# A build-time list scheduler for a fused chunk-attention and swish-MLP kernel, with other staging, transposes and rings for parts of its input

## The chip, the cores and the metric

The kernel runs on one core of one Trainium2 chip. The metric is device time in microseconds (us), median of several executions. The profile adds one execution that the hardware profiler recorded. An execution that is over 1.5% slower than the fastest of the same kernel is called slow here. Engines: PE is TensorE (matmul), PEld its weight load, DVE is VectorE, ACT is ScalarE, POOL is GpSimd, SP is SyncE. SP and ACT start DMA transfers; "SPq" is SP's instruction queue.

## The reference, cut to what matters

```
q, k, v: (8, 8, 576, 64) float32;  w_in: (512, 2048);  w_out: (2048, 512);  beta: (2048,)
# attention inside chunks of 64 positions
scores = 1/sqrt(64) * q_c @ k_c^T ;  attn = softmax(scores) ;  out = attn @ v_c
x = out.transpose(0, 2, 1, 3).reshape(4608, 512)
# MLP
h = x @ w_in
g = h * (1 / (1 + exp(-beta * h)))
y = g @ w_out                      # (4608, 512) float32
```

## The kernel before

The 4,608 tokens are nine blocks of 512. Block b is half-blocks 2b and 2b+1, so there are 18 half-blocks, 0 to 17. For each half-block: load q, k and v, cast them to bf16, transpose q and k, `scores`, `exp`, `attend`, normalize, transpose x. For each block: `mm1` (x times w_in, 16 tiles), `gate` (ACT and DVE), `mm2` (g times w_out, 16 tiles for each of four groups of 128 tokens), `keep_y` and the store. The attention of a later block and `mm2` of the block before are woven into `mm1` of a block.

Every engine has one queue that is fixed when the kernel is built and runs in order. An operation waits on semaphores for what it reads and for buffers that it overwrites, and everything behind it in that queue waits too. The order comes from a table of times written by hand:

```python
        events = []
        def at(time, fn, *args, **kw):
            events.append((time, len(events), fn, args, kw))
        def rest(h, tc, tt_, to, tv, ts, tx):          # attention with DMA transposes
            for w in range(2):
                at(tc + 1.0 * w, cast_qk, h, w, "pool")
                at(to + 2.0 * w, order, h, w, "pool")  # qkT -> qkO
            at(tt_, turn_dma, h)                       # on SP: qkb -> qkT
            ...
            at(ts, scores, h)
            ...
            at(tx, turn_x_dma, h)                      # on SP: xn -> xT
        for j in range(3):
            at((17, 20, 23)[j], load_w_out, j)         # into wstage, after w_in's casts
        ...
        events.sort(key=lambda e: (e[0], e[1]))
```

q and k of half-blocks 0 to 3 are transposed on PE, of all later ones by a DMA that SP starts (`turn_dma`); POOL then copies `qkT` to `qkO` in another order, and PE's `scores` reads `qkO`. The last block gathers the tails of eight sequences, so each of its two half-blocks needs 20 small loads instead of 6. And the output's DMAs are started by ACT.

The softmax here doesn't subtract the row's maximum and nothing guards it: scores larger than these inputs give would overflow.

## Time and profile before

The time was 360.49 us (median of 3, 357.36 to 363.85).

| from the profile before | |
|---|---|
| profiled span | 360.0 us |
| PE busy | 291.3 us (81%) |
| longest PE gap | 17.88 us, waiting for `qkO` |

The first lines of the page: busy time with share of the span, then PE, the granted clock and DMA in 40 equal slices, as tenths.

```profile
PE 291.3 (81%) x2466; PEld 142.1 (39%) x2498; DVE 141.2 (39%) x255; ACT 148.5 (41%) x230; POOL 122.6 (34%) x126
...
PE   1688977698696799999699969996999009899996
...
PEclk9999999899989999999789989998999757999999
DMA  8996999990962299269626962695244491312123
```

PE is the busiest engine, but it dips once in each block, and in slices 32 and 33 it does nothing. DMA, nearly full for the first 81 us, has a share of only about a half after that. So bandwidth is not, on the whole, what holds PE back after the start; waits are.

Waits of SP's queue and of PE: engine, line, what it waited for, total us, times, longest.

```profile
SPq L426 <- DVE g L464: 94.4, 11, 13.4
...
SPq L426 <- DVE xn L409: 23.8, 3, 13.3
```

```profile
PE A L370 <- POOL qkO L213: 26.3, 5, 17.9
```

SP stands for 94 us and 24 us before transposes of x (L426), and all loads behind them stand with it. PE loses 26 us to `qkO`, most of it once. The timelines of PE and SP show that once (start, duration, engine, line, operation; in brackets the idle time before it and what ended it):

```profile
278.04 1.03 PE L444 MATMUL F<-xT,w_in_bf 128*128 128x512 bf16 x4
296.95 0.64 PE L370 MATMUL A<-qkO 64*64 64x64 bf16 x32 [17.88 <-POOL qkO L213]
```

```profile
253.78 8.46 SPq L426 DMA_TRANSPOSE xT<-xn  x2
262.28 5.90 SPq L265 DMA_DIRECT2D qkstage<-in_q_dram  x8
268.22 5.72 SPq L265 DMA_DIRECT2D qkstage<-in_k_dram  x8
273.98 5.68 SPq L265 DMA_DIRECT2D qkstage<-in_q_dram  x8
279.71 5.69 SPq L265 DMA_DIRECT2D qkstage<-in_k_dram  x8
285.43 2.71 SPq L281 DMA_DIRECT2D vstage<-in_v_dram  x4
288.19 4.98 SPq L341 DMA_TRANSPOSE qkT<-qkb  x2
```

The last block's loads start only after the transposes of x, and SP needs 0.72 us for each. The transpose of q and k comes behind 36 of them at 288.2, POOL's copies come after it, and PE stands still until 297.

### The profile page before, as it was taken

The numbers are of one execution on the slowest core, as the hardware profiler recorded it, in microseconds if no ns is written. First come the engines' busy times: TensorE is split into PE (matmuls) and PEld (weight loads), VectorE is DVE, ScalarE is ACT, GpSimd is POOL, SyncE is SP. The second block draws the span as 40 slices with busy tenths as digits, with TensorE's granted clock in tenths as the row PEclk, the third lists the DMA queues.
The fourth block names the chain that finished last, engine by engine and source line by source line (L and its number), as shares of the span: only waits on it lengthen the run. The fifth ranks groups of instructions, "written<-read, shape, count | busy, mean of one in ns | idle before, by whom it ended". The sixth has DMA issues, their size and how long they took to land.

```text
span 360.0 us, 6004 instructions
## 1 busy us (share of the span) xinstructions
PE 291.3 (81%) x2466; PEld 142.1 (39%) x2498; DVE 141.2 (39%) x255; ACT 148.5 (41%) x230; POOL 122.6 (34%) x126
## 2 busy tenths in 40 slices
PE   1688977698696799999699969996999009899996
PEld 0563434475242344434243424343434004344444
DVE  1438631585125633453145415432543003534300
ACT  2437323684225635544344434343445003535421
POOL 1735362492180057314901480149002165000000
PEclk9999999899989999999789989998999757999999
DMA  8996999990962299269626962695244491312123
GB/s 228 352 353 198 348 304 251 216 267 8 184 132 58 69 268 219 59 175 270 142 53 159 275 158 59 196 271 119 60 121 120 128 196 33 78 32 56 31 58 87
DMA packets 101594, 57.54 MB, mean 160 GB/s; under 512 B 84024, under 2 KB 85312, under 8 KB 101568
## 3 DMA queue, kind: packets, MB, share of 16 engines
q1 hardware_dynamic: 93712, 47.33, 53.3%
q10 hardware_dynamic: 7856, 9.84, 10.3%
q8 instruction: 19, 0.31, 0.4%
q14 instruction: 7, 0.06, 0.1%
HBM read 36.71 MB, written 9.44 MB: 128 GB/s over the span
## 4 chain that ended last, share of the span: by engine, by line
PE 40%; DMA 16%; SPq 12%; DVE 12%; ACT 7%; POOL 5%; issue 3%; ACTq 3%; DVEq 0%
PE F L477 19%; PE F L444 11%; DMA qkT<-qkb 10%; DVE g L464 6%; SPq L265 6%; SPq L257 6%; POOL qkO L213 5%; DVE xn L409 3%; DMA qkstage<-in_k_dram 3%; ACT tt L461 3%; PE F L448 3%; ACTq L496 3%; PE A L444 3%; ACT E L379 3%; PE A L370 2%
## 5 line engine op out<-in xcount | busy, mean ns | idle before, releaser
L464 DVE SCALAR_TENSOR_TENSOR g<-tt,F 128x512 bf16<-128x512 bf16 (+1 forms) x148 | 91.8, 628 | 166.7 <-ACT tt L461 165.6
L477 PE MATMUL F<-w_out_bf,g 128*128 128x512 bf16 (+1 forms) x560 | 142.0, 381 | 5.8 <-issue 2.2
L461 ACT ACTIVATE tt<-F,beta_half 128x512 bf16<-128x512 f32 (+1 forms) x148 | 93.5, 641 | 127.0 <-PE F L444 104.4
L444 PE MATMUL F<-xT,w_in_bf 128*128 128x512 bf16 x448 | 117.9, 390 | 9.8 <-DVE g L464 6.4
L477 PEld LDWEIGHTS F<-w_out_bf,g 128*128 128x128 bf16 x592 | 56.3, 99 | 65.3 <-issue 3.5
L213 POOL CAST qkb<-qkstage 128x1024 bf16<-128x1024 f32 x33 | 34.2, 1040 | 117.0 <-DMA qkstage<-in_q_dram 90.6
L444 PEld LDWEIGHTS F<-xT,w_in_bf 128*128 128x128 bf16 x448 | 42.9, 100 | 69.5 <-DVE g L464 15.8
L213 POOL COPY qkO<-qkT 128x1024 bf16<-128x1024 bf16 x28 | 53.6, 1952 | 32.2 <-DMA qkT<-qkb 32.2
L370 PE MATMUL A<-qkO 64*64 64x64 bf16 x576 | 9.8, 208 | 34.2 <-POOL qkO L213 26.3
L379 ACT ACTIVATE E<-A 128x1024 bf16<-128x1024 f32 (+1 forms) x22 | 19.0, 865 | 34.0 <-PE A L370 34.0
L207 ACT ACTIVATE ostage<-F 128x512 f32<-128x512 f32 (+1 forms) x36 | 21.3, 591 | 23.0 <-PE F L477 20.4
L213 POOL CAST v_bf<-vstage 128x512 bf16<-128x512 f32 x36 | 21.6, 619 | 14.4 <-DMA vstage<-in_v_dram 14.1
L448 PE MATMUL F<-xT,w_in_bf 128*128 128x256 bf16 x160 | 23.2, 301 | 3.1 <-DVE g L464 1.7
L409 DVE TENSOR_TENSOR xn<-A,R 128x512 bf16<-128x512 f32 x36 | 24.9, 692 | 1.2
L370 PEld LDWEIGHTS A<-qkO 64*64 64x64 bf16 x576 | 7.2, 119 | 42.3 <-POOL qkO L213 28.8
L448 PEld LDWEIGHTS F<-xT,w_in_bf 128*128 128x128 bf16 x160 | 15.9, 106 | 7.5 <-DVE g L464 2.1
L407 DVE RECIPROCAL R<-A 128x8 f32<-128x8 f32 x36 | 7.2, 201 | 17.3 <-PE A L395 17.3
L444 PE MATMUL A<-xT,w_in_bf 128*128 128x512 bf16 x48 | 11.0, 380 | 1.7 <-DVE w_in_bf L213 1.7
L395 PEld LDWEIGHTS A<-v_bf,E 64*64 64x64 bf16 x576 | 7.3, 119 | 11.6 <-ACT E L379 4.1
L395 PE MATMUL A<-v_bf,E 64*64 64x65 bf16 x576 | 9.8, 208 | 2.2 <-ACT E L379 2.2
L323 PE MATMUL F<-ident,qkb 128*128 128x128 bf16 x32 | 4.2, 312 | 8.0 <-DVE qkb L213 8.0
L461 ACT ACTIVATE tt<-A,beta_half 128x512 bf16<-128x512 f32 x12 | 8.2, 687 | 3.3 <-PE A L444 3.3
(34 smaller groups left out, 64.0 us busy)
## 6 DMA issues: line engine op xcount, KB each, us to landing
out_dram<-ostage ACTq DMA_DIRECT2D x70, 128.0 KB, 3.4
qkstage<-in_q_dram SPq DMA_DIRECT2D x32, 256.0 KB, 5.2
qkstage<-in_k_dram SPq DMA_DIRECT2D x32, 256.0 KB, 5.2
vstage<-in_v_dram SPq DMA_DIRECT2D x30, 256.0 KB, 6.0
wstage<-in_moe_w_out_dram SPq DMA_DIRECT2D x4, 1024.0 KB, 7.5
wstage<-in_moe_w_in_dram SPq DMA_DIRECT2D x3, 1024.0 KB, 12.2
wstage<-in_moe_w_in_dram SPq DMA_DIRECT2D x2, 512.0 KB
qkstage<-in_q_dram SPq DMA_DIRECT2D x16, 64.0 KB
```

The costliest lines, as they stand in the source:

```text
L207: P.op("act", lambda e: e.activation(dst, src, AF.Copy, **kw), reads, writes)
L213: P.op(eng, lambda e: e.tensor_copy(dst, src), reads, writes, rows)
L257: return e.dma_start(qkstage[:, s, which, hb, :], src[blk][heads, 256 * hv:256 * hv + 256, :].rearrange("h (t i) d -> t h (i d)", i=8))
L265: return e.dma_start(qkstage[32 * c:32 * c + 32, s, which, hb, :], src[4 * hv + c][heads, S - 64:S, :].rearrange("h (t i) d -> t h (i d)", ...
L370: return e.matmul(bank(hb)[64 * c2:64 * c2 + 64, 64 * i:64 * i + 64], qkO[r, s, 1, hp, 64 * c:64 * c + 64], qkO[r, s, 0, hp, 64 * c:64 * c ...
L379: P.op("act", lambda e: e.activation(E[:, s, :, a:b, :].rearrange("p g i q -> p g (i q)"), A[:, 0:2, 64 * a:64 * b], AF.Exp, scale=0.125), ...
L409: P.op("dve", lambda e: e.tensor_tensor(xn[:, s, u, :, :, :].rearrange("p c k (h d) -> p c (k h) d", h=2), o[:, :, :, 0:64], R[:, 2 * u:2 ...
L444: return e.matmul(bank(n).rearrange("p (v c t) -> p v c t", v=2, c=4), w, xT[:, sx, :, u, :, 64 * hb:64 * hb + 64], start=(kt == 0), stop= ...
L448: return e.matmul(bank(n)[:, 256 * hv:256 * hv + 256].rearrange("p (c t) -> p c t", c=4), w, xT[:, sx, hv, u, :, 64 * hb:64 * hb + 64], st ...
L461: P.op("act", lambda e: e.activation(tt[:, T % 3, c], bank(n)[:, c], AF.Tanh, scale=beta_half[:, t:t + 1]), reads=[K("ps", n, v=("h", blk, ...
L464: P.op("dve", lambda e: e.scalar_tensor_tensor(g2[:, sg, t, c], tt[:, T % 3, c], 1.0, bank(n)[:, c], ALU.add, ALU.mult), reads=[K("ps", n, ...
L477: P.op("pe", lambda e, t=t: e.matmul(bank(n)[:, 0:b - a], g2[:, sg, t, 128 * s:128 * s + 128], w_out_bf[:, t, a:b], start=(t == 0), stop=( ...
```

## The change: its intent and the diff

The intent is to replace the times written by hand by a list scheduler that runs when the kernel is built. Each call gets a rank; loads and DMA transposes of q and k also form a "line" whose order is kept. The scheduler models every engine, the two DMA rings and the 16 DMA engines with fixed durations, lets each engine take the ready operation of lowest rank, and the order that results is the order of the queues. The chip still runs fixed queues; the model decides nothing at run time.

The diff, cut to its core (the long rest turns `at(...)` into `go(...)` and adds a duration to every operation; the `#` comments and the `...` at the ends of lines are put in here):

```diff
-        events.sort(key=lambda e: (e[0], e[1]))
-        for _, _, fn, args, kw in events:
-            fn(*args, **kw)
-        P.finish("sp")
+        P.schedule()        # list scheduling: "us" below are its modelled durations
         P.build()
 ...
+            P.dma("sp", (2.5, 128, 27), lambda e: e.dma_start_transpose(      # turn_dma
+                P.dma(queue, (0.62, 2, 92), lambda e, c=c: e.dma_start(       # last block's q, k
+            P.dma(queue, (0.6, 4, 92), lambda e: e.dma_start(                 # put
 ...
+        def stage_w_out(j):                                  # (a) was wstage[:, j]
+            if j == 0:
+                return vstage[:, 1, :, :, :].rearrange("p n h d -> p (n h d)"), ...
+            if j == 1:
+                return qkstage[:, 2, :, :, :].rearrange("p w b x -> p (w b x)"), ...
+            t0 = 8 * (j - 2)
+            return g2[:, 1, t0:t0 + 8, :].rearrange("p t d -> p (t d)").bitcast(F32), ...
 ...
+        load_half(0, "sp", "act")                            # (b) two rings
+        load_half(1, "sp", "act")
 ...
-        rest(4, 51, 53.2, 57.7, 57.5, 62, 65.5)
-        rest(5, 53, 57, 62, 61.8, 66.2, 69.5)
+        for h in (4, 5):                                     # (c) block 2 turned on PE
+            attention(h, "pe", (A0, A1), None, ("act", "dve"))
 ...
+        def stage_qk(h):                                     # (d) last block into wstage
+            if h < 2 * LAST:
+                return qkstage[:, h % NQ, :, :, :], ...
+            s = h % 2
+            return wstage[:, s, :].rearrange("p (w b x) -> p w b x", w=2, b=2), ...
 ...
+            at = None if h < 6 else 1000 + 10 * (h - 2)      # (e) load_half: place in SP's line
 ...
+                load(turn_dma, h, at=995 + 10 * h)           # its transposes, in the same line
 ...
+                go(r, scores, h, (0, 1), slack=0.5)
 ...
-        NOS = 3
+        NOS = 5                                              # output tiles in flight
 ...
+                go(0.5, put, blk, s, j, "sp")                # (f) stores from SP, were on ACT
```

A `slack` makes the model treat an operation's input as that much later than it is, so the operation gets a later place in its queue. It adds no wait.

## The prediction

> **What bounds the kernel now.** TensorE (PE) and the waits that starve it. In the table of busy time by stretch and PE's timeline, four 512-column matmuls start every 0.865 us in dense stretches, so 1,152 equivalents need about 249 us. Attention and PE transposes add about 18 us (estimate). The span is 360 us. The loss by stage:
>
> - blocks 0 and 1, 19.7 to 99.4 us: 80 us for about 58 us of PE work. DMA share 0.93, then 0.83. The w_out loads wait for the w_in staging buffers (issued 17.5 to 33 us, the fourth at 37); the data rate falls from about 350 to 198 GB/s. PE waits 3.2 us for transposed x at 99.4;
> - block 2, 99.4 to 126.8 us: 27 us for about 18.5;
> - blocks 3 to 6: 31, 36, 35 and 36 us; block 7: 48; block 8: 30; each has 27.7 us of matmuls plus about 1 us of attention. The DMA queue's waits show why: SP is in order, and the transposes of x wait 94 us in total behind gates of an earlier block, holding back the next loads. The largest PE gap is 17.9 us (279 to 297), waiting for qkO; in the chain, SP issues the last block's small loads one after another at 0.72 us. The clock there falls to 0.82; dense stretches run at 1.00. The Trainium skill, "TensorE: Matmul & The Clock Gate" (Part 1), says that idling halves the clock and activity restores it; the trace agrees (0.50 after that gap, 1.00 later), so filling gaps also removes slow matmuls.
>
> **What the change does.** It removes no matmul. (a) w_out gets its own staging, so loads stream without that gap. (b) The first two half-blocks load on two rings. The skill, "DMA: Bandwidth & Descriptors", says both share the same 16 engines, so I expect 1 to 2 us. (c) Block 2 is turned on PE: +1.6 us of PE, against DMA transposes of 4.5 to 7.3 us and POOL copies of 1.95 us. (d) The last block's 40 loads go into free staging well ahead: removes nearly all of the 17.9 us. (e) Loads no longer sit behind blocked transposes: removes 2.5 to 8 us in each of blocks 3 to 7. (f) Output issues leave ACT (0.6 us each) and go to SP.
>
> **Sum (estimates from the durations above).** Loads through half-block 5 plus both weights are about 17 MB; DMA takes until about 57 us. Block 2 starts near 80 (was 99.4), block 3 near 100 (was 126.8). Six blocks at 29.2 us end at 275. Final matmuls 14, last store 4: 293. I add 9 us of stalls, because a static order made from modelled durations drifts from real ones, and DMA would be busy about 25 us of each 29: **302 us, range 290 to 318**. Faster by over 2%: 0.96; within 2%: 0.03; slower: 0.01.
>
> **What would show it.** Block 2's first mm1 near 80 us; blocks 3 to 8 at 28.5 to 30.5 us each; no PE gap over 3 us after 100 us; PE waits on qkO falling from 26 us to under 4; PE busy over 90% of the span; mean clock 0.97 or more; no 94 us of x-transpose waits; w_out issued without the gap.
>
> **What would make it wrong.** DMA near saturation stretching transposes so that PE waits for x every block (then 320 to 335); an SP order that differs from real readiness; early loading slower than estimated; or better, if stalls are near zero (about 290).

## The result, and the profile after

The kernel with the change took **321.98 us** (median of 4, 320.96 to 323.29), against 359.83 (4 runs, 357.36 to 363.85) for the kernel before in the same rounds. The ratio is 0.897, 95% interval 0.891 to 0.903. A ratio is the mean time of one kernel's fast runs over that of the other's fast runs of the same rounds, so it is not quite the ratio of the medians quoted. The change is 38 us faster, and 20 us slower than predicted, outside the range.

```profile
PE 289.6 (90%) x2546; PEld 144.0 (45%) x2546; DVE 143.4 (45%) x263; ACT 152.5 (47%) x241; POOL 114.4 (36%) x119
...
PE   0679998998999999899999999599399999999994
...
PEclk9999999999999999999999999879779999999999
DMA  6999199989999999999999559539901521111133
```

PE's busy time is the same as before, its idle time fell from 68.7 to 31.9 us. The dips of each block are gone, but slices 26 and 29 (5 and 3 tenths) are new holes, with a lower clock around them, and DMA has a hole in slice 5 (1 tenth).

The same stretch table for the kernel after; columns are the stretch, its length, busy us (and instructions) of PE, PEld, DVE, ACT, POOL, then the granted clock, DMA share and GB/s:

```profile
core 0: us, PE busy (x) PEld busy (x) DVE busy (x) ACT busy (x) POOL busy (x), PEclk, DMA share, GB/s
32.00:40.00 8.00, 8.00 (x39) 3.63 (x37) 7.08 (x15) 5.05 (x8) 2.35 (x4) 1.00 0.09 33
...
199.00:235.00 36.00, 26.65 (x193) 11.34 (x192) 10.17 (x17) 12.01 (x18) 15.94 (x12) 0.83 0.71 144
235.00:322.00 87.00, 82.45 (x484) 38.45 (x482) 30.55 (x48) 35.55 (x54) 0.00 (x0) 0.99 0.22 49
```

From 199 to 235 us PE idles 9.4 us and is granted 0.83 of its clock, with DMA far from full. After that PE is nearly always busy. The waits of SP and of PE:

```profile
SPq L641 <- ACT ostage L319: 64.2, 16, 9.7
SPq L482 <- POOL v_bf L321: 32.7, 11, 5.5
SPq L253 <- POOL w_out_bf L321: 13.8, 1, 13.8
...
SPq L385 <- DVE w_out_bf L321: 4.4, 1, 4.4
```

```profile
PE A L513 <- POOL qkO L321: 9.3, 2, 5.7
PE F L468 <- DVE qkb L321: 8.3, 1, 8.3
```

SP's 94 us before transposes of x are gone; it now waits to start stores (L641), most of it late in the kernel, when little else is left to issue (62 of the 64 us come after 222 us), and for w_out's casts early on. The 32.7 us at L482, the transposes of q and k, were there before as well (32.1 us). The list puts them down to POOL's cast of v, on which the kernel does not make a transpose depend; such releasers are inferred, and what holds these issues stays open. PE's waits for `qkO` fell from 26.3 to 9.3 us, in two gaps; the other line, 8.3 us, is the very start of the kernel. PE's timeline at the two gaps:

```profile
202.79 1.03 PE L591 MATMUL F<-xT,w_in_bf 128*128 128x512 bf16 x4
207.43 0.64 PE L513 MATMUL A<-qkO 64*64 64x64 bf16 x32 [3.61 <-POOL qkO L321]
208.00 1.89 PE L620 MATMUL F<-w_out_bf,g 128*128 128x512 bf16 x4
...
223.78 1.03 PE L591 MATMUL F<-xT,w_in_bf 128*128 128x512 bf16 x4
230.54 0.64 PE L513 MATMUL A<-qkO 64*64 64x64 bf16 x32 [5.73 <-POOL qkO L321]
```

The two operations that wait are `scores` of half-blocks 15 and 16. After each gap four matmuls take 1.89 us instead of 1.03: PE runs at half clock until 212.8 and 236.7. And this is what SP did while PE came to the first gap:

```profile
171.00 5.95 SPq L482 DMA_TRANSPOSE qkT<-qkb  x1
176.99 1.24 SPq L641 DMA_DIRECT2D out_dram<-ostage  x2
178.27 3.06 SPq L391 DMA_DIRECT2D wstage<-in_q_dram  x4
181.37 2.82 SPq L391 DMA_DIRECT2D wstage<-in_k_dram  x4
184.23 1.27 SPq L573 DMA_TRANSPOSE xT<-xn  x1
185.55 0.68 SPq L391 DMA_DIRECT2D wstage<-in_q_dram  x1
186.27 1.16 SPq L641 DMA_DIRECT2D out_dram<-ostage  x2
187.48 2.23 SPq L391 DMA_DIRECT2D wstage<-in_q_dram  x3
189.75 2.82 SPq L391 DMA_DIRECT2D wstage<-in_k_dram  x4
192.61 0.68 SPq L405 DMA_DIRECT2D wstage<-in_v_dram  x1
193.34 1.34 SPq L573 DMA_TRANSPOSE xT<-xn  x1
194.73 1.32 SPq L641 DMA_DIRECT2D out_dram<-ostage  x2
196.09 2.05 SPq L405 DMA_DIRECT2D wstage<-in_v_dram  x3
198.18 3.38 SPq L482 DMA_TRANSPOSE qkT<-qkb  x1
```

SP hardly waits for data here. The last cast that transpose 14 reads ended at 161.2 us, and that of transpose 15 at 175.8, 22 us before its issue (the casts in the order of POOL's queue). Between the transposes of half-blocks 14 (171.0) and 15 (198.2) it starts 20 loads of the last block (14.3 us), six stores (3.7 us) and two transposes of x (2.6 us). The next 20 loads stand in the same way before transpose 16 at 221.8. From its issue to `scores` transpose 15 needs 9.2 us (5.3 for the DMA, 3.8 for POOL's two copies), so `scores` of 15 starts at 207.4. PE had reached it at 203.8.

To see where time is lost, I took the start times of all matmuls and subtracted from each step the time that this kind takes in dense stretches (0.216 us for 512 columns, 0.108 for 256, 0.056 for 128, 0.0084 for the small ones of attention). This "loss" holds waits and half-clock time alike:

| stage, after | work, us | loss, us |
|---|---|---|
| before the first matmul | | 8.3 |
| 8.3 to 80.7 us | 52.8 | 19.8 |
| 80.7 to 199 us | 111.8 | 6.4 |
| 199 to 235 us | 21.3 | **14.9** |
| 235 us to the last matmul | 80.6 | 1.2 |
| all | 266.5 | 50.6, and 4.2 after the last matmul |

Of the 14.9 us, 9.7 come before `scores`; nearly all of the rest is half clock. The Trainium skill, "TensorE: Matmul & The Clock Gate" (section "Why this matters for your kernels"), says to leave no PE idle gap above about 3 us between bursts, or the clock falls. The traces agree in kind: the 3.61 us gap was followed by 5.3 us of slow matmuls, and the one 2.0 us gap of run e1 below by none. But in the kernel before, gaps of 2.76, 2.69 and 2.57 us (ending at 175.7, 211.9 and 246.8 us) were each followed by half clock too, so 3 us is not a safe limit.

### The profile page after: what moved, and what is told of

Read it like the earlier page. It is cut to its first block, busy times and chain, and to the rows that moved or that the text cites. A ratio compares the mean times of both kernels' runs of the same rounds, so it can differ in the third digit from the quotient of the medians.

```text
span 321.5 us, 6150 instructions
## 1 busy us (share of the span) xinstructions
PE 289.6 (90%) x2546; PEld 144.0 (45%) x2546; DVE 143.4 (45%) x263; ACT 152.5 (47%) x241; POOL 114.4 (36%) x119
## 4 chain that ended last, share of the span: by engine, by line
PE 80%; DVE 6%; DMA 6%; POOL 2%; ACT 2%; SPq 2%; issue 1%; DVEq 0%
PE F L620 37%; PE F L591 27%; PE F L595 4%; DVE xn L552 3%; PE A L591 3%; DMA qkT<-qkb 3%; PE A L513 3%; POOL qkO L321 2%; PE A L538 2%; DMA qkstage<-in_q_dram 2%; PE A L560 1%; PE A L468 1%; PE F L468 1%; DVE g L611 1%; DVE R L550 1%; ACT E L522 1%
## 5 line engine op out<-in xcount | busy, mean ns | idle before, releaser
L591 PE MATMUL F<-xT,w_in_bf 128*128 128x512 bf16 x448 | 113.4, 384 | 2.0 <-DVE g L611 1.9
L620 PEld LDWEIGHTS F<-w_out_bf,g 128*128 128x128 bf16 x592 | 57.0, 99 | 65.3 <-issue 3.3
L591 PEld LDWEIGHTS F<-xT,w_in_bf 128*128 128x128 bf16 x448 | 42.4, 99 | 55.6 <-DVE g L611 9.5
L321 POOL COPY qkO<-qkT 128x1024 bf16<-128x1024 bf16 x24 | 46.4, 1964 | 22.4 <-DMA qkT<-qkb 18.4
L321 POOL CAST qkb<-qkstage 128x1024 bf16<-128x1024 f32 x30 | 30.8, 1044 | 28.8 <-DMA qkstage<-in_q_dram 22.6
L319 ACT ACTIVATE ostage<-F 128x512 f32<-128x512 f32 (+1 forms) x36 | 21.3, 592 | 33.1 <-PE F L620 33.1
L321 POOL CAST v_bf<-vstage 128x512 bf16<-128x512 f32 x32 | 19.7, 617 | 25.7 <-DMA vstage<-in_v_dram 25.3
L522 ACT ACTIVATE E<-A 128x512 bf16<-128x512 f32 (+1 forms) x24 | 19.4, 810 | 17.5 <-PE A L513 17.5
L595 PE MATMUL F<-xT,w_in_bf 128*128 128x256 bf16 x160 | 22.0, 289 | 0.0
L595 PEld LDWEIGHTS F<-xT,w_in_bf 128*128 128x128 bf16 x160 | 15.6, 104 | 2.7
L321 POOL CAST qkb<-wstage 128x1024 bf16<-128x1024 f32 x4 | 4.2, 1042 | 20.7 <-DMA wstage<-in_q_dram 15.5
```

The lines of the kernel that those rows point to most:

```text
L319: P.op("act", us, lambda e: e.activation(dst, src, AF.Copy, **kw), reads, writes)
L321: P.op(eng, us, lambda e: e.tensor_copy(dst, src), reads, writes)
L522: P.op("act", act_us(128 * (b - a)), lambda e: e.activation(E[:, s, :, a:b, :].rearrange("p g i q -> p g (i q)"), A[:, 0:2, 64 * a:64 * b] ...
L591: return e.matmul(bank(n).rearrange("p (v c t) -> p v c t", v=2, c=4), w, xT[:, sx, :, u, :, 64 * hb:64 * hb + 64], start=(kt == 0), stop= ...
L595: return e.matmul(bank(n)[:, 256 * hv:256 * hv + 256].rearrange("p (c t) -> p c t", c=4), w, xT[:, sx, hv, u, :, 64 * hb:64 * hb + 64], st ...
L620: P.op("pe", 0.2158 * (b - a) / 512, lambda e, t=t: e.matmul(bank(n)[:, 0:b - a], g2[:, sg, t, 128 * s:128 * s + 128], w_out_bf[:, t, a:b] ...
```

## The experiments

Theory A: PE's queue holds `scores` of half-blocks 15 and 16 earlier than their `qkO` can exist, because SP's in-order queue issues their transposes late, behind the last block's loads and the stores; the static order, made with shorter modelled times, turns SP's lateness into PE waits. Rivals: the data are late because DMA is short of bandwidth; the hole at 32 to 40 us starves the rest; PE's own order does not matter because what follows needs the same data anyway.

Running only the kernel's own scheduler shows its belief: it places `scores` of 15 at 198.8 and of 16 at 213.1 us, and a span of 300.4 us. That is a plan and no measurement; the chip ran them at 207.4 and 230.5. Where a run below is said to change the order of a queue, the queues that the two kernels' schedulers build were compared in this way too.

### e5_late_scores: PE's order, for three operations

```diff
-                go(r, scores, h, (0, 1), slack=0.5)
+                go(r, scores, h, (0, 1), slack={15: 6, 16: 13, 17: 6}.get(h, 0.5))
```

> Only the place of three groups of score matmuls (half-blocks 15, 16, 17) in PE's fixed order changes; no load, transpose or output is touched. Theory A (PE's order, made from a model that has the transposes of q and k some 9 and 17 us too early, waits although other matmuls are ready): the gaps of 3.6 and 5.7 us before the scores and the two half-clock stretches of 6.8 us go, and the time falls by 13 to 17 us, to about 305 to 309 us. Theory B (DMA is saturated there, so that data are truly late for the block that needs them): the wait only moves to a later matmul and the time stays within 3 us of 322.

Measured: **309.84 us** (309.25 to 310.21), ratio 0.862 [0.856, 0.868]. The fall of 12.1 us is a little less than the 13 to 17 expected. In the queues, what moved is these scores with what hangs on them (`exp`, `attend`, normalize and the transposes of x) and one group of `mm2`; loads, stores and transposes of q and k keep their order among themselves. The transposes were issued nearly as late (195.9 and 219.1 us). PE now does other matmuls first. The first line is PE's `scores` of 15, without a wait; the second is the stretch table:

```profile
210.79 0.45 PE L513 MATMUL A<-qkO 64*64 64x64 bf16 x32
```

```profile
199.00:235.00 36.00, 36.00 (x257) 16.33 (x256) 15.64 (x25) 18.90 (x29) 15.04 (x11) 1.00 0.63 137
```

The loss from 199 to 235 us fell from 14.9 to 0.6 us, and 12 us of time went with it. So the data were in time for what needs them; only the order made PE wait. The bandwidth rival falls, and so does the one that says that PE's order doesn't matter.

### e1_turn_first: SP's order

```diff
             at = None if h < 6 else 1000 + 10 * (h - 2)
+            if h >= 2 * LAST:
+                at = 996 + 10 * (h - 1)
```

This puts transposes 15 and 16 ahead of the last block's loads.

> The transposes of half-blocks 15 and 16 are issued ahead of the last block's 20 loads each, instead of behind them. Theory A (loads of the last block, about 0.72 us each on the in-order SP queue, hold the transposes back): transpose 15 is issued near 178 us instead of 198, the first gap (3.6 us) and its half-clock stretch go; transpose 16 is issued near 203 instead of 222, so the second gap shrinks to 0 to 4 us; time 307 to 315 us. Theory B (saturated DMA): the transposes land no earlier, both gaps stay, 319 to 324 us.

Measured: **314.89 us** (311.57 to 316.5; the run of 316.5 is slow, and the median of the other three is 314.07), ratio 0.877 [0.870, 0.885]. SP's timeline, transposes 15 to 17:

```profile
180.31 2.21 SPq L482 DMA_TRANSPOSE qkT<-qkb  x1
202.37 2.66 SPq L482 DMA_TRANSPOSE qkT<-qkb  x1
226.50 3.01 SPq L482 DMA_TRANSPOSE qkT<-qkb  x1
```

Transpose 15 comes 18 us earlier than in the change, 16 comes 19 us earlier. What is left is one wait of 2.0 us, before `scores` of 17. PE's queue changed here too: the scheduler, which now expects the data sooner, puts `scores` of 15 and 16 earlier (behind 748 and 820 matmuls of the MLP, 788 and 852 in the change), and still PE does not wait for them. The lateness can be cured from either end, on SP or on PE.

### e6_old_stage: undo the staging of step (d)

```diff
-            if h < 2 * LAST:
+            if True:
```

in `stage_qk` and `stage_v`, so the last block uses the old buffers.

> The last block is staged in the buffers of the other blocks again, as before the change; the order of all queues stays. If the free staging is what moved its loads up, they start later than 178 us and the largest gap grows again by 5 us or more (327 us and up). If the order of the SP queue sets their time (they start at 178 us though the staging is free from about 36 us), nothing changes: 320 to 324 us, the same gaps of about 3.6 and 5.7 us.

Measured: 323.48 us (321.08 to 324.35), ratio 0.899, waits for `qkO` 9.7 us, no difference that the runs resolve. The scheduler builds the same five queues, operation for operation. The free staging alone did nothing: the loads' place in SP's line, and not a free buffer, set their time. In the change the last cast out of `wstage` ends at 32.4 us, yet the loads start at 178.3.

### e8_recal: measured costs in the scheduler's model

```diff
-            P.dma("sp", (2.5, 128, 27), lambda e: e.dma_start_transpose(
+            P.dma("sp", (3.8, 128, 27), lambda e: e.dma_start_transpose(
-                P.dma(queue, (0.62, 2, 92), lambda e, c=c: e.dma_start(
+                P.dma(queue, (0.72, 2, 92), lambda e, c=c: e.dma_start(
```

and alike for the other loads (from 0.62 to between 0.65 and 0.72) and the stores (0.60 to 0.64).

> Only numbers of the build-time model change: what one issue on SP costs, set to what the trace after the change shows (transposes of q and k 3.8 us instead of 2.5, loads of the last block 0.72 instead of 0.62, other loads 0.65 to 0.70, outputs 0.64 instead of 0.60). The list scheduler then orders the same work by itself. Theory A (the order is bad because these costs were too low): the model's own times of the last three score groups move 7 to 11 us later, PE no longer waits over 2 us for qkO after 190 us, 307 to 312 us. If the issue costs are not what misled it, the gaps of 3.6 and 5.7 us stay: 318 to 323 us.

Measured: 315.9 us (314.81 to 316.33), ratio 0.880 [0.874, 0.886]. One wait of 4.3 us for `qkO` stays, that of half-block 15. This misses the expectation: right mean costs give half of the gain. The new plan has `scores` of 16 and 17 11 us later, but those of 15 only 1.0 us later (199.8 instead of 198.8), which fits the wait that stays. The model still knows nothing of SP's issues that are held up: single loads that mostly take 0.60 us took up to 3.43 us while DMA was full, and the transposes ranged from 2.0 to 5.95 us.

### e4_wout_own: the early hole in DMA

The hole at 32 to 40 us: w_out's pieces 0 and 1 borrow buffers of half-block 2, so its loads wait for w_out's casts (the lines of 13.8 and 4.4 us above; SP idles from 20.2 to 38.5 us).

```diff
             if j == 0:
-                return vstage[:, 1, :, :, :]...
+                return qkT[:, :, :, :, :].rearrange("p s w i t -> p (s w i t)").bitcast(F32), ...
             if j == 1:
-                return qkstage[:, 2, :, :, :]...
+                return ostage[:, 0:4, :].rearrange("p n d -> p (n d)"), ...
```

> The first two pieces of w_out are staged in buffers that nobody needs yet (qkT, ostage) instead of those of half-blocks 2 and 3. Theory A: the hole of about 7 us in the DMA traffic (31 to 38.5 us, data rate 33 GB/s) goes, the load of half-block 2 is issued near 21 us instead of 38.5, PE's losses between 36 and 81 us fall from 8.7 to about 5 us, and the whole stream of loads runs about 7 us earlier, so that the late gaps shrink too: 310 to 316 us. If early loading is limited by something else, block 1 starts no earlier and the time stays within 3 us of 322.

Measured: 317.76 us (317.27 to 318.35), ratio 0.884 [0.878, 0.890], a miss by 1.8 us. The hole is gone, as the same stretch shows:

```profile
32.00:40.00 8.00, 8.00 (x39) 3.62 (x37) 8.00 (x13) 5.06 (x8) 5.14 (x7) 1.00 0.99 276
```

The loss up to 80.7 us did not fall (20.1 against 19.8), but the first matmul came at 6.7 us instead of 8.3; both together, PE is 1.3 us ahead by then. (Such a difference can be chance: e6 has the same queues as the change, and its first matmul came at 6.1 us.) What fell clearly is the late loss, from 14.9 to 10.8: one gap of 7.4 us instead of two, so one half-clock stretch instead of two. PE's order of the scores is the same, and transposes 15 and 16 were issued 5.5 and 5.9 us earlier: enough for the first gap, not for the second. So the hole explains at most 4 of the 15 us.

### e10_wout_wstage: undo step (a)

w_out goes back into `wstage`, each piece after the cast of w_in from the same buffer.

```diff
-            if j == 0:
-                return vstage[:, 1, ...
-            ...
+            return wstage[:, j, :], \
+                [("wst", j, x, c, hb) for x in range(2) for c in range(4) for hb in range(2)]
```

> Undoes one part of the change: w_out is staged in the buffers of w_in again and waits for their casts. If the staging apart is worth what the prediction gave it (a share of the 20 us gained before block 2), 325 us or more. If its own wait (half-block 2 behind the casts of w_out) cancels it, nothing changes: 318 to 324 us, with the DMA hole only moved from 31-38 us to about 20-27 us.

Measured: **318.15 us** (316.89 to 319.59), ratio 0.887 [0.881, 0.893]. Undoing this part makes the kernel nearly 4 us faster; the intervals of the two ratios just overlap, so the size is uncertain. DMA's share from 32 to 40 us is 1.04 instead of 0.09, and the hole expected at 20 to 27 us is not there (share 0.99). As built, the new staging moves the hole (in the kernel before a share of 0.67 from 24 to 32 us) and deepens it instead of closing it. PE's two late waits are 2 and 7.3 us here, again with one half-clock stretch (clock 0.91 from 199 to 235 us, against 0.83).

### e9_blk2_dma: undo step (c)

```diff
-            attention(h, "pe", (A0, A1), None, ("act", "dve"))
+            attention(h, "dma", None, None, None)
```

for half-blocks 4 and 5.

> Undoes one part of the change: block 2 is turned by DMA and POOL again instead of PE. The prediction's cost sheet: saves 1.6 us of PE, adds two transposes of q and k and two of x to a DMA stream and SP queue that are full from 40 to 176 us. Theory A: block 2's first full mm1 starts some 15 us later than now (near 103 instead of 88 us) and the time rises to 330 to 340 us. If turning on PE only trades PE work for DMA work, 319 to 325 us.

Measured: **334.75 us** (332.2 to 336.06), ratio 0.932 [0.925, 0.939]. PE's timeline at block 2's first `mm1`, and the stretch of block 2, which in the change had 45.11 us busy at clock 1.00:

```profile
106.58 4.00 PE L591 MATMUL F<-xT,w_in_bf 128*128 128x512 bf16 x9 [8.69 <-DMA xT<-xn]
```

```profile
80.70:126.00 45.30, 29.84 (x389) 13.30 (x390) 15.39 (x29) 16.27 (x24) 28.23 (x24) 0.81 1.00 227
```

PE waits for x that is transposed by DMA. DMA is full in this stretch (share 1.00), but it is in the change as well (1.03), so whether the full DMA or SP's order makes the transpose late is not shown. (This trace lacks some matmul records, so its busy time is low; the wait and the clock do not depend on them.) Turning block 2 on PE is worth about 13 us.

### e7_early_slack: the order of the early attention

e5 and besides 0.6 us of slack for PE's attention steps of half-blocks 2 to 5.

```diff
-                    go(r, scores, h, (u,))
+                    go(r, scores, h, (u,), slack=0 if h < 2 else 0.6)
```

and alike for `turn_pe`, `attend` and `turn_x_pe`.

> The late-scores version (309.8 us), with 0.6 us of slack also for PE's attention steps of blocks 1 and 2 (half-blocks 2 to 5). If PE's losses of about 5 us between 56 and 81 us (waits of 0.5 to 0.9 us for the normalised x, for qkO and for the exponentials) come from an order that is a little too optimistic, as the late ones do, they fall to 2 us or less and the time to 305 to 308 us. If they are the length of the attention chain itself, the time stays at 308 to 311 us.

Measured: 309.57 us (308.3 to 310.63), the same as e5. The early loss is not cured by moving these steps by this much. Whether another order would do it, I did not try.

### e2_puts_act: undo step (f)

```diff
-                go(0.5, put, blk, s, j, "sp")
+                go(0.5, put, blk, s, j, "act")
```

> Undo part f alone: the output's DMA issues go back from SP to ACT. Theory A (PE waits in a fixed order for transposes that SP issues late, because SP's in-order queue is full of issues and of waits for the output's tiles): SP loses 64 us of waits for ostage and about 46 us of issuing, transposes 15 and 16 are issued earlier than 198 and 222 us, the late loss falls from 14.9 to under 9 us, 315 to 319 us. Rival (SP's share in the issuing does not matter, only the last block's loads do): 322 plus or minus 1.5 us, or slower, if ACT's own work (casts, copies from PSUM) is held up by 0.6 us for each output.

Measured: **311.37 us** (309.98 to 311.76), ratio 0.865 [0.861, 0.868], better than expected. SP's timeline, transposes 15 and 16:

```profile
185.30 4.14 SPq L482 DMA_TRANSPOSE qkT<-qkb  x1
...
205.90 2.84 SPq L482 DMA_TRANSPOSE qkT<-qkb  x1
```

They come 13 and 16 us earlier than in the change, and the loss from 199 to 235 us is 1.2 us. The scheduler also planned PE's queue anew, but it put `scores` of 15 and 16 earlier (behind 772 and 828 matmuls of the MLP, 788 and 852 in the change), which by itself would make PE wait longer. So the gain comes from SP's time.

### e12_acts_late and best3_all: do the gains add?

e12 joins e2's line with e5's; best3 adds e4's buffers.

> Output issues on ACT and, as in the run with late scores, the scores of half-blocks 15, 16 and 17 later in PE's order. If the output issues on SP cost only through the late gap (theory A), the two gains do not add: 309 to 312 us, beside 311.4 and 309.8 of each alone. Rival (SP's time for output is a cost of its own, also in the early and middle stages): they add, under 306 us.

> Output issues on ACT, later scores, and w_out pieces 0 and 1 staged in qkT and ostage. Theory A: no better than the run with later scores and that staging (307.2): 306.5 to 310. Rival: under 303 us.

Measured: e12 309.98 us (308.8 to 311.24), best3 307.82 us (307.2 to 308.26). The gains do not add: 309.8 with later scores, 311.4 with the stores on ACT, 310.0 with both. So the stores on SP cost through the same gap, and nothing that the runs resolve besides.

### e11_one_ring: undo step (b)

```diff
-        load_half(0, "sp", "act")
-        load_half(1, "sp", "act")
+        load_half(0, "sp", "sp")
+        load_half(1, "sp", "sp")
```

> Undo part b alone: half-blocks 0 and 1 load on SP's ring only. The prediction's step b says 1 to 2 us: 322.5 to 324 us, with the first matmul 1 to 2 us later than 8.3 us. Rival (the early DMA is not what PE waits for after block 0, as the run with w_out in other buffers suggested): 322 plus or minus 1 us.

Measured: 323.61 us (322.17 to 324.59), ratio 0.898 [0.894, 0.903], beside 0.897 [0.891, 0.903] of the change: no difference that the runs resolve. The first matmul starts at 6.8 us, earlier than the change's 8.3; the prediction's step would have it later. Nothing follows from this, as e6, with the change's own queues, started at 6.1 us.

### best1_late_wout and best2_turn_wout: the best of it together

best1 is e5's line and e4's buffers. best2 is e1's lines, e4's buffers and `slack={15: 3, 16: 6, 17: 5}`.

> Both mends together: the scores of half-blocks 15, 16 and 17 later in PE's order, and w_out pieces 0 and 1 staged in qkT and ostage. If the gain of the w_out buffers (4.2 us alone) came from the early stage it adds to that of the order: about 306 us. If it came from the late gap (my reading: the early loss fell by only 1.4 us), the order has already removed that: 308 to 309.5 us, beside 309.8 of the order alone.

> As best1, with transposes 15 and 16 also ahead of the last block's loads in SP's order, and scores of 15, 16, 17 later by 3, 6 and 5 units. Expected 305.5 to 309 us: the late loss under 1 us, the last block's loads land in time as in the run with the transposes first. If the last block's loads now come late, a gap of 2 us or more before the scores of half-block 17 and 310 us or more.

Measured: **307.17 us** (305.97 to 307.94), ratio 0.853 [0.850, 0.857], and **307.08 us** (306.54 to 307.69), ratio 0.853 [0.850, 0.857]. Both beat both kernels; against the change it is about 15 us. best1 lies between its two expectations: 2.7 us better than e5. Its loss up to 80.7 us is 17.7 us, against 20.7 in e5 (first matmul at 7.9 and 8.0 us), so with the late gap gone a part of the hole's cost does appear early. The intervals of the two runs' ratios just overlap, so the size is uncertain.

| | us | loss 199 to 235 us |
|---|---|---|
| before | 359.8 | |
| the change | 322.0 | 14.9 |
| stores on ACT (e2) | 311.4 | 1.2 |
| transposes first on SP (e1; fast runs) | 314.1 | 2.6 |
| later scores on PE (e5) | 309.8 | 0.6 |
| later scores and other w_out buffers (best1) | 307.2 | 0.8 |

## Why the prediction was right or wrong

**The direction and most of the mechanism were right; the time was 20 us too low.** Step by step:

- **The sum.** 302 us with 266.5 us of PE work, 8.3 before the first matmul and 4.2 after the last leaves 23 us for all losses (worked out here; the prediction gave no list): 9 of "stalls", about 4 in six blocks at 29.2 us, and about 10 before block 3's start at 100 us, by when 81.5 us of PE work should be done. Measured were 42.3 us: 20.7 until that much work was done (at 109.6 us), and 21.6 after. So the early part was undersized by some 10 us, and the later part by some 9.
- **The failing step: "I add 9 us of stalls, because a static order made from modelled durations drifts from real ones".** The mechanism is the right one, the size is not. One stretch of 36 us, 199 to 235, alone lost 14.9 us to two waits for `qkO` and the half clock after them. e5 moved three operations in PE's order, and 12 us came back, which alone brings the time inside the range. The prediction's list of what would make it wrong had named this: "an SP order that differs from real readiness".
- **A coincidence.** The measured 322 us lies in the 320 to 335 that the prediction set for a nearly saturated DMA with PE waiting for x in every block. That is luck: among the change's PE waits there is none for a transpose of x by DMA.
- **Step (d), "well ahead: removes nearly all of the 17.9 us", was wrong.** The staging is free, but the loads stayed where their rank puts them in SP's line, between transposes 14, 15 and 16. The 17.9 us gap went, and the same loads made two new gaps of 3.6 and 5.7 us, each with a half-clock stretch. e6 shows that the staging itself was worth nothing. I read the new buffer as an earlier load; the line in `load_half` that sets the rank was in the diff.
- **Step (f) was named but not costed.** Stores take SP 0.6 us each. In e2, taking them away brought 10.6 us, by way of the same gap. I counted what ACT gains and not what SP loses.
- **Step (e) was right about the 94 us.** SP no longer stands before transposes of x. What it did not see is the mirror image: transposes now stand behind loads and stores.
- **Step (a) was wrong as built.** The first three w_out pieces are issued without a gap, but they occupy half-block 2's buffers, and DMA's share fell to 0.09 for 8 us instead. Undoing it (e10) is faster by nearly 4 us.
- **Step (b), 1 to 2 us, is not confirmed.** e11 resolves no difference. The Trainium skill, "DMA: Bandwidth & Descriptors" (section "Issuing engines are not separate DMA queues"), says that transfers from any engine share the same 16 DMA engines; the run is in accord with it: over the first 20 us the DMA share was 0.89 with one ring and 0.94 with two.
- **Step (c) was only costed (+1.6 us of PE).** Its gain, about 13 us by e9, was folded into the early starts.
- **The early starts were late, the second failing step.** Block 2's first `mm1` came at 87.8 us, not 80, and block 3's at 125.2, not 100 (though `mm1` of block 2 is woven with `mm2` of block 1, so these starts count different work than before). Of the 19.8 us lost up to 80.7, 11.2 came before 25 us, more than the 10 implied for the whole early part, and the kernel before has much the same there (11.6). Nearly 6 of them are slow matmuls: a step of 256 columns took 0.213 us up to 25 us and 0.110 after, although the profile's clock, whose record begins at 25 us, shows 1.00; the rest are waits inside attention's chain on PE, ACT and DVE. e4, e7 and best1 show that neither the DMA hole (1 to 3 us) nor these steps' slack explains most of the early loss. What would shorten it stays open.
- **The signs.** Right: PE busy at 90%, clock 0.979, no 94 us of waits for x. Wrong: no gap over 3 us (two), waits for `qkO` under 4 us (9.3), and 28.5 to 30.5 us for each of blocks 3 to 8 (block 6 took 46.2 from its first `mm1` to that of block 7, 202.8 to 249.0).

## What to carry to other kernels

A scheduler that runs at build time hands its model's errors to every in-order queue: check on the trace which operations of the busiest engine wait, and give just those a later place, which cost nothing here and was worth 12 us. When a buffer is freed or a DMA moved to another engine, ask what place its issue gets in that engine's queue and what stands behind it. And a gap costs more than its length when it is long enough to lower the clock: 9.3 us of waits lost 14.9 us here.

## What the Trainium skill lacked or had wrong

- "DMA: Bandwidth & Descriptors", section "Issuing engines are not separate DMA queues": spreading DMAs over engines saves only the sequencer's time, "which is usually small relative to the DMA itself". e11 is in accord with the sharing. But 40 small loads at 0.72 us and 12 stores at 0.6 us took SP some 36 of the 46 us from 176 to 222, while the DMA share was 0.61; moving the stores to ACT saved 10.6 us (e2). This page does not say that on a full in-order queue this time delays the transfers behind it; "Perfetto Trace Analysis" (section "DMA Optimizations") comes nearer: balancing DMAs over the issuing engines may help when issuing is the limit.
- The same page: for a DMA transpose it gives only sequencer cycles of "previous generations", in a part on trn3, and for a load while the DMA engines are full I found no issue time. The change's trace shows 2.0 to 5.95 us of SP for one transpose of q and k, and up to 3.43 us for a load that otherwise takes 0.60. What holds the longer ones stays open.
- "TensorE: Matmul & The Clock Gate", section "Part 1: The HAM clock gate": full clock returns after at least one busy window of about 3.4 us. After the change's two gaps the half clock lasted longer than that one window: 5.3 us (after the gap of 3.6) and 6.1 us (after 5.7), counted from the first matmul after the gap; the clock record has 6.83 us both times, and 3.41 us after two of the shorter gaps of the kernel before. The page's words "at least" allow for it, but an estimate with 3.4 us can be too low.
- The same page, section "Why this matters for your kernels": its limit of about 3 us for an idle gap is too high for this case. In the kernel before, gaps of 2.57 to 2.76 us were followed by half clock (0.50 from 246.7 to 250.1 us at the one of 2.57); gaps of 2.0 us (e1 and e10) were not.
